# Turning expert 2's rows beside expert 1's first layer in an attention and mixture-of-experts kernel

## The chip, the cores and the metric

The kernel runs on one core of a Trainium2 chip. The metric is device time in microseconds (us), one launch. Engines in this text: TensorE (PE) multiplies, VectorE (DVE) and ScalarE (ACT) work on tiles, GpSimd (POOL) issues the indirect transfers, SyncE (SP) issues the others.

## The reference

A decayed linear attention over 4 x 8 heads and 768 positions gives `x` with 3072 tokens of 512. A noisy gate picks two of eight experts for each token, and each expert is a two-layer network:

```python
for e in range(E):
    for k in range(2):
        mask = top2[:, k] == e
        h = np.maximum(x[mask] @ w1[e], 0.0)
        out[mask] += top2_w[mask, k, None] * (h @ w2[e])
```

`w1[e]` is 512 x 1024, `w2[e]` 1024 x 512. Everything is fp32.

## The kernel before, in words

Attention, gate and routing come first; expert 0 is begun beside them. Then experts 1 to 7 run one after the other. An fp32 product is made of three products of split operands (high x high, high x low, low x high), so weights and activations are split into two parts: the high one by ScalarE, the low one by VectorE.

An expert has up to seven tiles of rows: six of 128, and a tail of 64 or 32 rows. Tiles 0 to 3 make the wide part, tiles 4 to 6 the narrow one. `parts` orders them: expert 1 does the wide part first, later experts the narrow one (`tile_order(2)` is 4, 5, 6, 0, 1, 2, 3). The loop at line 1133 runs the first layer: for each part eight blocks `f` of 128 hidden columns, each 12 matmuls into a bank `pS` (four of them) and an eviction with relu, ScalarE first (line 863), then VectorE (line 867). The loop at line 1161 runs the second layer, `gemm2`: for each tile 24 matmuls (16 for the tail) into `pO` or `pKV` by turns, an eviction by VectorE (line 907) into a buffer `ot`, and a scatter to `out` by POOL.

The rows of the next expert come on this way, with one tile `xg` per row tile:

- `gather_rows`: POOL gathers the tokens' rows of `x` into `xg` (line 810), by lists that `prepare` loads with `load_rec` (line 801).
- `turn_rows`: VectorE transposes 32 x 32 blocks into a buffer `ot` (line 829), and SyncE stores it to `turned` in DRAM (line 831). The pool `ot` has three buffers, shared with the evictions of the second layer.
- `fetch_rows`: four SyncE transfers bring the blocks back transposed into `xg` (line 836).
- `split_rows`: ScalarE writes the high part `xth` (line 843), VectorE the low part `xtl` (line 844).

Each engine and SyncE's queue works in the order in which the program issues. From expert 2 on, turning and fetching lie in the wide half of the first layer, and splitting in the second layer. Expert 1's successor is different: its rows are gathered in expert 1's narrow half (line 1155), and turned, fetched and split in its second layer (lines 1169 to 1174), a fetch one tile behind its turn. Weight loads share SyncE: in step `t` of the second layer, `split_w(1, e + 1, t)` splits a piece of the next expert's first weights and `load_w(2, e + 1, t)` loads a piece of its second ones into the buffer `wst` set free. The last row tile of expert 2 (`late`) is fetched after the second layer and split inside expert 2's own first layer (line 1143).

Beside all that VectorE computes a small table for overflowing rows (`ovj`), a step at a time, on lines 1081 to 1117.

Of the kernel before, what the change touches and what calls it, by code (L numbers as in the profile page):

```python
# [39 lines left out]
FB = F // 128  # L40
# [38 lines left out]
def tiles(e):  # L79

    return NT if TAILS[e] else NT - 1


def size(e, t):
    return TS if t < NT - 1 else TAILS[e]


def sub(ap, offset, dims):
    return bass.AP(tensor=ap.tensor, offset=ap.offset + offset, ap=dims)
# [27 lines left out]
def kernel(  # L117
# [557 lines left out]
    def xt(part, c):  # L675

        i = c.start >= TX * TS
        return XT[part][i][:, :, c.start - i * TX * TS:c.stop - i * TX * TS]
# [95 lines left out]
    def parts(e):  # L774
        if not e:
            return [(sum(PARTS0[:i]), n) for i, n in enumerate(PARTS0)]
        n = PARTS1 if TAILS[e] else PARTS2
        return [(0, n[0]), (n[0], n[1])] if e == 1 else [(n[0], n[1]), (0, n[0])]

    def tile_order(e):  # L780

        return [t0 + t for t0, n in parts(e) for t in range(n)]
# [11 lines left out]
    def load_rec(e, i, queue=nc.sync):  # L794

        t0, n, size = list(lists(e))[i]
        nm = f"{i}{size}" if e else f"z{i}"
        r = rp.tile([size, n, RW], I32, name="rec" + nm, bufs=3 if e else 1)
        if e:
            rows = lst[bass.ds(ROW[e] + t0 * TS, n * size), :]  # L800
            queue.dma_start(r.rearrange("p n w -> p (n w)"), rows.rearrange("(p n) w -> p (n w)", p=size))
        else:
            ld = queue.dma_start(r, sub(lst, t0 * TS * RW, [[n * RW, size], [1, n * RW]]))
            if i < NG - 1:
                lst_ld.append((i, ld))
        for j in range(n):
            REC[e, t0 + j] = r[:, j, :]
    def gather_rows(e, t, rows=NTOK):
        at = REC[e, t][:, 0:1] if e else IDX[t // 2][:, t % 2:t % 2 + 1]
        nc.gpsimd.indirect_dma_start(  # L810
            out=XG[t][:size(e, t)], out_offset=None, in_=x_tok[:rows, :],
            in_offset=bass.IndirectOffsetOnAxis(ap=at, axis=0),
            bounds_check=rows - 1, oob_is_err=False)
# [12 lines left out]
    def turn_rows(t, n):  # L826

        tr = hp.tile([TS, DM], FT, name="ot", bufs=3)[:n, :]
        nc.vector.transpose(tr.rearrange("p (i d c) -> p i d c", d=DB, c=32),
                            XG[t][:n, :].rearrange("p (d i c) -> p i d c", d=DB, c=32))  # L830
        nc.sync.dma_start(turned[t][:n, :], tr)

    def fetch_rows(t, n):

        for i in range(4):
            nc.sync.dma_start(XG[t][i * 32:(i + 1) * 32, :4 * n].rearrange("r (b x) -> r b x", x=128),  # L836
                              sub(turned[t], i * 128, [[DM, 32], [32 * DM, n // 32], [1, 128]]))

    def split_rows(t, n):

        p = XG[t][:, :4 * n].rearrange("p (b d c) -> p d b c", d=DB, c=32)
        hi, lo = [xt(i, slice(t * TS, t * TS + n)).rearrange("p d (b c) -> p d b c", c=32) for i in range(2)]
        nc.scalar.activation(hi, p, AF.Copy)  # L843
        nc.vector.tensor_tensor(lo, p, hi.bitcast(FT), op=SUB)  # L844

    def gemm1(e, t0, n, f):
        evac1(e, t0, n, f, mm1(e, t0, n, f))

    def columns(e, t0, n):
        return slice(t0 * TS, min((t0 + n) * TS, FULL + TAILS[e]))  # L850
# [19 lines left out]
    def ht(e, part, f, c):  # L870

        at = c.start + (0 if not part else TAILS[e] if c.start >= FULL else CAP + TAIL)
        return HT[0][:, f, at:at + c.stop - c.start]
# [10 lines left out]
    def gemm2(e, t, between=None):  # L884
        n = size(e, t)
        cs = slice(t * TS, t * TS + n)
        p = psum.tile([128, DM], FT, name=("pO", "pKV")[next(turn) % 2])
        terms = [(f, a, b) for f in range(FB) for a, b in ((0, 0), (0, 1), (1, 0))]
        o = hp.tile([TS, DM], FT, name="ot", bufs=3) if e else PV[t]
        w, pv = REC[e, t][:, 1:2].bitcast(FT), PV[t][:n, :]  # L890
        if n == TS:
            for i, (f, a, b) in enumerate(terms):
                if between and i == MID:
                    between()
                nc.tensor.matmul(p, ht(e, a, f, cs), W2[b][f // 2][:, f % 2, :], start=(i == 0),  # L895
                                 stop=(i == len(terms) - 1))
        else:
            for i in range(2 * FB):
                f, b = i // 2, i % 2
                nc.tensor.matmul(p[:2 * n, :], HT[0][:, f, FULL:FULL + 2 * n], W2[b][f // 2][:, f % 2, :],  # L900
                                 start=(i == 0), stop=(i == 2 * FB - 1))
            o = o[:n, :]
            nc.scalar.activation(o, p[n:2 * n, :], AF.Copy)
            nc.vector.tensor_add(o, o, p[:n, :])
            p = o
        if e:
            nc.vector.scalar_tensor_tensor(o, p, w, pv, op0=MULT, op1=ADD)  # L907
            scatter_out(e, t, o)
        else:
            nc.vector.tensor_scalar(o, p, w, None, op0=MULT)  # L910

    def scatter_out(e, t, o):
        nc.gpsimd.memset(spacer, 0.0)
        st = nc.gpsimd.indirect_dma_start(  # L914
            out=out, out_offset=bass.IndirectOffsetOnAxis(ap=REC[e, t][:, 0:1], axis=0), in_=o, in_offset=None,
            bounds_check=NTOK - 1, oob_is_err=False)
        if t == 0:
            out_st.clear()
        for s in out_st:
            tc.declare_no_dep(st.ins, s.ins, reason="an expert has a token once")  # L920
        out_st.append(st)
# [199 lines left out]
    def prepare(e):  # L1121

        which_expert(e, nc.sync)
        which_list(e, nc.sync)
        for i, _ in enumerate(lists(e)):
            load_rec(e, i)

    for e in range(1, E):
        if e == E - 1:
            n_over = nc.values_load(ntot[0:1, 0:1], min_val=0, max_val=MAXOV)  # L1130
        if e == 1:
            prepare(2)
        for i, (t0, n) in enumerate(parts(e)):
            for f in range(FB):
                gemm1(e, t0, n, f)
                if e == 1 and f >= 4:
                    next(ovj, None)
                if e > 1 and i and e + 1 < E:
                    if 1 <= f <= tiles(e + 1):
                        fetch_rows(f - 1, size(e + 1, f - 1))  # L1140
                    if f < tiles(e + 1):
                        turn_rows(f, size(e + 1, f))
                if e == 2 and not i and f == 1:
                    split_rows(late, size(2, late))
                    gather_rows(3, late)
                if i == 0 and f % 2 == 0:
                    split_w(2, e, f // 2)
                if i == 0 and f % 2 and e + 1 < E:
                    load_w(1, e + 1, f // 2)
                if (t0 == 0 or e == 1) and f < tiles(e):  # L1150
                    nc.gpsimd.tensor_copy(spacer, ht(e, 0, f, columns(e, t0, n))[0:1, 0:1].bitcast(FT))  # L1151
                    if t0 == 0:
                        gather_prev(e, f)
                    else:
                        gather_rows(2, tile_order(2)[f])
        if e == E - 1:
            nc.gpsimd.drain()
        if e + 2 < E:
            prepare(e + 2)
        nxt = tile_order(e + 1) if e + 1 < E else []  # L1160
        for t in range(tiles(e)):
            gemm2(e, t)
            if e == 1:
                next(ovj, None)
            if e + 1 < E:
                if t < 4:
                    split_w(1, e + 1, t)
                    load_w(2, e + 1, t)
                for j in nxt[t - 1:t] if e == 1 and t else ():
                    fetch_rows(j, size(2, j))  # L1170
                for j in nxt[t:t + 1] if e == 1 else ():
                    turn_rows(j, size(2, j))
                for j in (nxt[t - 1:t] if t else ()) if e == 1 else nxt[t:t + 1]:
                    split_rows(j, size(e + 1, j))
                    if e + 2 < E and j < tiles(e + 2):
                        gather_rows(e + 2, j)
        if e == 1:
            late = nxt[-1]
            fetch_rows(late, size(2, late))
    with tc.For_i(0, n_over) as it:  # L1180
        e_r = nc.sync.value_load(tab[0:1, 0, bass.ds(it, 1)], min_val=0, max_val=E - 1)
        row = nc.sync.value_load(tab[0:1, 1, bass.ds(it, 1)], min_val=0, max_val=E * STRIDE - OV)
# [59 lines left out]
```

## Time and profile before

| | before |
|---|---|
| median of 3 runs | 738.89 us (736.31 to 739.82) |
| profiled execution, own time | 741.05 us |
| its span, first to last instruction | 739.3 us |
| TensorE busy | 706.7 us, 96% |
| VectorE busy | 357.6 us, 48% |
| ScalarE busy | 237.0 us, 32% |
| POOL busy | 274.9 us, 37% |
| mean granted TensorE clock | 0.989 of full speed |

The span starts at 0 in every view. A wait is the idle time of an engine just before an instruction, with the instruction that ended it. TensorE is busy nearly everywhere, so the places where it is not are to be found in its waits and its timeline; the other engines matter where TensorE waits for them. For a transfer the row shows its issue; the time to landing comes apart.

### The profile page before, as it was taken

What the parts mean: (1) busy time and instruction counts of PE and PEld (TensorE: products, weight loads), DVE (VectorE), ACT (ScalarE), POOL (GpSimd) and SP (SyncE); (2) the same over time, 40 slices, a digit from 0 to 9 for tenths busy, and PEclk for the clock granted to TensorE, in tenths of its full rate; (3) what the DMA queues carried; (4) which work ended last, traced back from release to release, by engine and by line L of the source; (5) the groups of instructions that cost most, each with busy time, mean ns of one, the idle gap of its engine ahead of it and who ended that gap; (6) DMA issues with size and microseconds to landing.
All of it is one profiled execution on the core that took longest, in us unless ns stands there. A gap on an engine that the chain in (4) does not pass through costs nothing.

```text
span 739.3 us, 13508 instructions
## 1 busy us (share of the span) xinstructions
PE 706.7 (96%) x4917; PEld 601.7 (81%) x4917; DVE 357.6 (48%) x815; ACT 237.0 (32%) x451; POOL 274.9 (37%) x439
## 2 busy tenths in 40 slices
PE   8899998899999999769999999999999999999996
PEld 6788886699888887658888887988798898889885
DVE  6335869777235543455436433644353544335211
ACT  1567685331133320142214221423042322224200
POOL 3200336677756442323252415242512433221311
PEclk9999999999999999989999999999999999999999
DMA  7999997981527636457464636564655556550211
GB/s 162 204 230 232 245 255 210 272 243 39 114 62 264 185 87 195 141 156 217 147 222 138 178 129 228 158 187 145 208 150 178 193 173 180 161 166 14 79 43 38
DMA packets 139594, 122.50 MB, mean 166 GB/s; under 512 B 88554, under 2 KB 107370, under 8 KB 139524
## 3 DMA queue, kind: packets, MB, share of 16 engines
q1 hardware_dynamic: 124996, 85.22, 43.7%
q0 software_dynamic: 13104, 36.34, 15.6%
q8 instruction: 40, 0.66, 0.4%
q14 instruction: 30, 0.25, 0.1%
q10 hardware_dynamic: 1424, 0.04, 0.1%
HBM read 87.15 MB, written 35.55 MB: 166 GB/s over the span
## 4 chain that ended last, share of the span: by engine, by line
PE 75%; DMA 9%; issue 6%; DVE 4%; ACT 2%; SPq 2%; POOL 1%; POOLq 0%; ACTq 0%; DVEq 0%
PE pS L857 34%; PE pKV L895 14%; PE pO L895 12%; DMA wst<-in_moe_w_dram 3%; DMA xg<-turned 2%; PE pS L356 2%; PE pKV L369 2%; PE pO L369 2%; PE pO L900 1%; PE pS L326 1%; PE pS L429 1%; SPq L836 1%; PE pS L401 1%; POOL out_dram L914 1%; DMA qt<-in_q_dram 1%
## 5 line engine op out<-in xcount | busy, mean ns | idle before, releaser
L857 PE MATMUL pS<-xth,w1h 128*128 128x512 f32 (+3 forms) x544 | 182.0, 335 | 7.7 <-DVE ht L867 5.8
L857 PE MATMUL pS<-xtl,w1h 128*128 128x512 f32 (+3 forms) x544 | 181.3, 333 | 0.4 <-DVE xtl L822 0.4
L857 PE MATMUL pS<-xth,w1l 128*128 128x512 f32 (+3 forms) x544 | 181.1, 333 | 0.0
L863 ACT ACTIVATE ht<-pS 128x512 fp32r<-128x512 f32 (+3 forms) x136 | 65.6, 483 | 218.7 <-PE pS L857 213.0
L867 DVE SCALAR_TENSOR_TENSOR ht<-pS,ht 128x256 fp32r<-128x256 f32 (+3 forms) x176 | 76.5, 455 | 112.1 <-ACT ht L863 110.1
L895 PE MATMUL pO<-w2h,ht 128*128 128x512 f32 x384 | 124.1, 394 | 3.9 <-DVE ot L907 3.9
L895 PE MATMUL pKV<-w2h,ht 128*128 128x512 f32 x384 | 123.0, 391 | 0.0
L857 PEld LDWEIGHTS pS<-xth,w1h 128*128 128x128 f32 x544 | 103.5, 190 | 17.6 <-ACT ht L863 6.0
L857 PEld LDWEIGHTS pS<-xtl,w1h 128*128 128x128 f32 x544 | 103.5, 190 | 9.4 <-DVE xtl L822 0.7
L857 PEld LDWEIGHTS pS<-xth,w1l 128*128 128x128 f32 x544 | 103.5, 190 | 8.9
L914 POOL DMA_INDIRECT out_dram<-ot,rec x46 | 59.2, 1286 | 118.3 <-DVE ot L907 110.3
L895 PEld LDWEIGHTS pO<-w2h,ht 128*128 128x128 f32 x384 | 72.8, 190 | 20.7 <-DVE ot L907 4.3
L895 PEld LDWEIGHTS pKV<-w2h,ht 128*128 128x128 f32 x384 | 72.1, 188 | 16.2
L810 POOL DMA_INDIRECT xg<-x_tok,rec x46 | 49.4, 1074 | 91.3 <-DVE xtl L844 45.5
L895 PE MATMUL pO<-w2l,ht 128*128 128x512 f32 x192 | 76.0, 396 | 0.0
L895 PE MATMUL pKV<-w2l,ht 128*128 128x512 f32 x192 | 75.4, 393 | 0.0
L879 POOL DMA_INDIRECT pv<-out_dram,rec x46 | 47.1, 1023 | 31.7 <-issue 25.2
L843 ACT ACTIVATE xth<-xg 128x512 fp32r<-128x512 f32 (+1 forms) x39 | 22.4, 598 | 105.5 <-DMA xg<-turned 105.5
L622 POOL DMA_INDIRECT lst<-recs,dest x48 | 47.7, 993 | 13.6 <-issue 9.0
L844 DVE TENSOR_TENSOR xtl<-xg,xth 128x512 fp32r<-128x512 f32 (+1 forms) x39 | 25.6, 656 | 46.7 <-ACT xth L843 46.7
L1151 POOL COPY spacer<-ht 1x1 f32<-1x1 f32 x53 | 9.4, 177 | 99.6 <-ACT ht L863 99.5
L907 DVE SCALAR_TENSOR_TENSOR ot<-pKV,rec,pv 128x512 f32<-128x512 f32 x21 | 15.8, 750 | 59.8 <-PE pKV L895 57.1
(228 smaller groups left out, 932.3 us busy)
## 6 DMA issues: line engine op xcount, KB each, us to landing
wst<-in_moe_w_dram SPq DMA_DIRECT2D x48, 512.0 KB, 4.6
turned<-ot SPq DMA_DIRECT2D x36, 256.0 KB, 3.1
xg<-turned SPq DMA_DIRECT2D x144, 64.0 KB, 2.1
wst<-in_moe_w_dram SPq DMA_DIRECT2D x32, 256.0 KB, 4.0
kt<-in_k_dram SPq DMA_DIRECT2D x24, 256.0 KB, 5.2
qt<-in_q_dram SPq DMA_DIRECT2D x24, 256.0 KB, 5.5
vt<-in_v_dram SPq DMA_DIRECT2D x24, 256.0 KB, 5.3
x_tok<-xc SPq DMA_DIRECT2D x12, 512.0 KB, 5.4
```

What stands on the lines that cost most here:

```text
L369: nc.tensor.matmul(PO[u][a][half(g), hp, :], lhs, rhs, start=n == 1, stop=n == (8 if u % NW or a else 4))
L622: st = nc.gpsimd.indirect_dma_start(out=lst, out_offset=bass.IndirectOffsetOnAxis(ap=r["dest"][:, i, c:c + 1], axis=0), in_=r["rec"][:, c, ...
L810: nc.gpsimd.indirect_dma_start(out=XG[t][:size(e, t)], out_offset=None, in_=x_tok[:rows, :], in_offset=bass.IndirectOffsetOnAxis(ap=at, ax ...
L843: nc.scalar.activation(hi, p, AF.Copy)
L844: nc.vector.tensor_tensor(lo, p, hi.bitcast(FT), op=SUB)
L857: nc.tensor.matmul(p, W1[a][d][:, fs], xt(b, cs)[:, d], start=(d == 0 and i == 0), stop=(d == DB - 1 and i == 2))
L863: nc.scalar.activation(ht(e, 0, f, cs), p, AF.Relu)
L867: nc.vector.scalar_tensor_tensor(ht(e, 1, f, c), p[:, r], 0.0, ht(e, 0, f, c).bitcast(FT), op0=OP.max, op1=SUB)
L879: nc.gpsimd.indirect_dma_start(out=PV[t][:size(e, t), :], out_offset=None, in_=out, in_offset=bass.IndirectOffsetOnAxis(ap=REC[e, t][:, 0: ...
L895: nc.tensor.matmul(p, ht(e, a, f, cs), W2[b][f // 2][:, f % 2, :], start=(i == 0), stop=(i == len(terms) - 1))
L907: nc.vector.scalar_tensor_tensor(o, p, w, pv, op0=MULT, op1=ADD)
L914: st = nc.gpsimd.indirect_dma_start(out=out, out_offset=bass.IndirectOffsetOnAxis(ap=REC[e, t][:, 0:1], axis=0), in_=o, in_offset=None, bo ...
```

## The change

Expert 2's rows are turned from block 3 (`LAG`) of expert 1's narrow half on. `turn_next(k)` fetches the row tile at place `k - 2` of `tile_order(2)` and turns the one at place `k`. It is called after blocks 3 to 7 (k = 0 to 4) and ahead of each tile of expert 1's second layer (k = 5 and on). Each row tile is now split one step earlier in the second layer, as for later experts, the last one in its last step; the steps for `late` are gone.

```diff
--- before.py
+++ after.py
@@ -1125,6 +1125,16 @@
         for i, _ in enumerate(lists(e)):
             load_rec(e, i)
 
+    LAG = 3
+
+    def turn_next(k):
+
+        js = tile_order(2)
+        for j in js[k - 2:k - 1] if k >= 2 else ():
+            fetch_rows(j, size(2, j))
+        for j in js[k:k + 1]:
+            turn_rows(j, size(2, j))
+
     for e in range(1, E):
         if e == E - 1:
             n_over = nc.values_load(ntot[0:1, 0:1], min_val=0, max_val=MAXOV)
@@ -1140,9 +1150,8 @@
                         fetch_rows(f - 1, size(e + 1, f - 1))
                     if f < tiles(e + 1):
                         turn_rows(f, size(e + 1, f))
-                if e == 2 and not i and f == 1:
-                    split_rows(late, size(2, late))
-                    gather_rows(3, late)
+                if e == 1 and i and f >= LAG:
+                    turn_next(f - LAG)
                 if i == 0 and f % 2 == 0:
                     split_w(2, e, f // 2)
                 if i == 0 and f % 2 and e + 1 < E:
@@ -1159,6 +1168,8 @@
             prepare(e + 2)
         nxt = tile_order(e + 1) if e + 1 < E else []
         for t in range(tiles(e)):
+            if e == 1:
+                turn_next(t + FB - LAG)
             gemm2(e, t)
             if e == 1:
                 next(ovj, None)
@@ -1166,17 +1177,10 @@
                 if t < 4:
                     split_w(1, e + 1, t)
                     load_w(2, e + 1, t)
-                for j in nxt[t - 1:t] if e == 1 and t else ():
-                    fetch_rows(j, size(2, j))
-                for j in nxt[t:t + 1] if e == 1 else ():
-                    turn_rows(j, size(2, j))
-                for j in (nxt[t - 1:t] if t else ()) if e == 1 else nxt[t:t + 1]:
+                for j in nxt[t:t + 1]:
                     split_rows(j, size(e + 1, j))
                     if e + 2 < E and j < tiles(e + 2):
                         gather_rows(e + 2, j)
-        if e == 1:
-            late = nxt[-1]
-            fetch_rows(late, size(2, late))
     with tc.For_i(0, n_over) as it:
         e_r = nc.sync.value_load(tab[0:1, 0, bass.ds(it, 1)], min_val=0, max_val=E - 1)
         row = nc.sync.value_load(tab[0:1, 1, bass.ds(it, 1)], min_val=0, max_val=E * STRIDE - OV)
```

SyncE's queue in expert 1's second layer before, from the first store on (`wst` is a weight piece, `turned_364` the stored tile 4, `xg_2430` its place in SBUF, 365 and 2432 tile 5):

```order
L831 DMA turned_364<-ot 128x512
L748 ISA
L748 DMA wst<-in_moe_w_dram 128x2x512
L836 DMA xg_2430<-turned_364 32x4x128 x4
L831 DMA turned_365<-ot 128x512
L748 ISA
L748 DMA wst<-in_moe_w_dram 128x2x512
L836 DMA xg_2432<-turned_365 32x4x128 x4
```

and the changed kernel's, from the same store, which now lies in the first layer's narrow half:

```order
L831 DMA turned_364<-ot 128x512
L831 DMA turned_365<-ot 128x512
L836 DMA xg_2430<-turned_364 32x4x128 x4
L831 DMA turned_366<-ot 32x512
L836 DMA xg_2432<-turned_365 32x4x128 x4
L831 DMA turned_360<-ot 128x512
L836 DMA xg_2434<-turned_366 32x128 x4
L831 DMA turned_361<-ot 128x512
```

The stores and the first three fetches now come in a row, ahead of the lists of expert 3 and of the four weight loads that stood between them. After the lists follow fetch and store alternately with the weight loads: fetches four and five of `xg` stand ahead of the first and second weight load.

VectorE in expert 1's narrow half, blocks 3 and 4 (line 867 evicts, 1091 and 1093 are the table):

```order
 L867 SCALAR_TENSOR_TENSOR ht<-pS,ht 128x256
 L867 SCALAR_TENSOR_TENSOR ht<-pS,ht 128x64
+L829 STREAM_TRANSPOSE ot<-xg_2430 128x512
 L867 SCALAR_TENSOR_TENSOR ht<-pS,ht 128x256
 L867 SCALAR_TENSOR_TENSOR ht<-pS,ht 128x64
 L1091 COPY ov_3463<-ov_3462 1x8
 L1093 TENSOR_TENSOR ov_3463<-ov_3463,ov_3462 1x1 x4
+L829 STREAM_TRANSPOSE ot<-xg_2432 128x512
```

A turn stands behind the eviction and the table step of its block, and ahead of the next block's eviction.

VectorE in the second step of expert 1's second layer (line 907 is the tile's eviction, 772 the weight split, 844 a row split):

```order
 L907 SCALAR_TENSOR_TENSOR ot<-pO,rec_3186,pv_2425 128x512
 L1104 TENSOR_REDUCE ovt<-ovg 1x40
 L772 TENSOR_TENSOR w1l_334<-wst,w1h_330 128x1024
-L829 STREAM_TRANSPOSE ot<-xg_2432 128x512
-L844 TENSOR_TENSOR xtl_348<-xg_2430,xth_346 128x4x128
+L844 TENSOR_TENSOR xtl_348<-xg_2432,xth_346 128x4x128
 L907 SCALAR_TENSOR_TENSOR ot<-pKV,rec_3186,pv_2427 128x512
```

The turn is gone from here, and the row split is that of the next row tile, a step earlier than before.

## Rows read from the trace of the kernel before

**Rows 1.** The waits of TensorE, whole run: engine, line, releaser: total us, times, longest.

```profile
PE pS L857 <- DVE ht L867: 5.8, 1, 5.8
...
PE pO L895 <- DVE ot L907: 3.9, 1, 3.9
...
PE pKV L900 <- DVE ot L907: 1.6, 1, 1.6
PE pS L857 <- ACT w2h L768: 1.5, 1, 1.5
```

**Rows 2.** Timeline of TensorE, 252.7 to 404.8: start, us, line, operation.

```profile
252.79 0.30 PE L857 MATMUL pS<-xth,w1h 128*128 128x320 f32 x1
...
266.87 0.40 PE L895 MATMUL pKV<-w2h,ht 128*128 128x512 f32 x1
...
311.21 0.29 PE L857 MATMUL pS<-xth,w1h 128*128 128x288 f32 x1
...
333.43 0.39 PE L857 MATMUL pS<-xth,w1h 128*128 128x512 f32 x1
...
355.20 0.39 PE L895 MATMUL pO<-w2h,ht 128*128 128x512 f32 x1
...
391.82 0.29 PE L857 MATMUL pS<-xth,w1h 128*128 128x288 f32 x1
...
404.46 0.39 PE L857 MATMUL pS<-xth,w1h 128*128 128x512 f32 x1
```

**Rows 3.** Windows: us, busy PE, PEld, DVE, ACT, POOL, PEclk, DMA share, GB/s.

```profile
303.50:333.40 29.90, 20.96 (x122) 18.95 (x122) 14.57 (x32) 9.53 (x17) 8.25 (x11) 0.89 0.53 162
355.20:391.80 36.60, 36.60 (x161) 29.19 (x160) 13.70 (x18) 7.54 (x11) 14.37 (x18) 1.00 0.53 177
```

**Rows 4.** Timeline of VectorE, expert 1's second layer.

```profile
287.11 0.69 DVE L844 TENSOR_TENSOR xtl<-xg,xth 128x512 fp32r<-128x512 f32 x1 [6.16 <-ACT xth L843]
...
297.02 0.69 DVE L844 TENSOR_TENSOR xtl<-xg,xth 128x512 fp32r<-128x512 f32 x1 [6.42 <-ACT xth L843]
```

**Rows 5.** Timeline of SyncE, expert 1's second layer.

```profile
290.01 0.41 SPq L748 DMA_DIRECT2D wst<-in_moe_w_dram  x1
290.53 1.92 SPq L836 DMA_DIRECT2D xg<-turned  x4
292.56 0.42 SPq L831 DMA_DIRECT2D turned<-ot  x1
```

**Rows 6.** Timeline of ScalarE, the last row tiles.

```profile
321.56 0.63 ACT L843 ACTIVATE xth<-xg 128x512 fp32r<-128x512 f32 x1 [4.64 <-DMA xg<-turned]
```

**Rows 7.** Timeline of VectorE, a turn in expert 2's wide half.

```profile
337.60 0.70 DVE L829 STREAM_TRANSPOSE ot<-xg 128x512 f32<-128x512 f32 x1
```

**Rows 8.** Timeline of VectorE, expert 1's narrow half.

```profile
262.31 0.56 DVE L867 SCALAR_TENSOR_TENSOR ht<-pS,ht 128x256 fp32r<-128x256 f32 x2 [1.21 <-ACT ht L863]
...
262.96 0.71 DVE L1093 TENSOR_TENSOR ov<-ov,ov 1x1 f32<-1x1 f32 x4
```

**Rows 9.** Timeline of POOL, expert 1's narrow half.

```profile
256.16 1.05 POOL L810 DMA_INDIRECT xg<-x_tok,rec  x1 [0.61 <-issue]
```

**Rows 10.** Transfers into `xg`, 255 to 270.

```profile
DMA to landing us min/median/max: 3.4/3.5/3.5
```

**Rows 11.** Transfers into `pv`, 333 to 356, expert 2's wide half.

```profile
DMA to landing us min/median/max: 2.9/3.9/4.4
```

**Rows 12.** Timeline of SyncE, expert 2's second layer.

```profile
368.05 1.71 SPq L836 DMA_DIRECT2D xg<-turned  x4
371.18 1.53 SPq L801 DMA_DIRECT2D rec<-lst  x3
372.91 6.76 SPq L748 DMA_DIRECT2D wst<-in_moe_w_dram  x4
```

**Rows 13.** Transfers to and from `turned`, 262 to 325.

```profile
DMA to landing us min/median/max: 1.8/3.7/5.0
```

**Rows 14.** Transfers into `wst`, 266 to 300.

```profile
DMA to landing us min/median/max: 4.3/4.3/4.3
```

## The prediction

> **What bounds the kernel now.** I read the waits of TensorE first. It is busy for almost the whole span, so only what stops it can be won. Its longest waits are few, and four of them are neighbours: 5.8, 3.9, 1.6 and 1.5 us [rows 1]. The timeline of TensorE puts all four between expert 1's second layer and the end of expert 2's first pass: the second layer starts at 266.87, expert 2's narrow half at 311.21, its wide half at 333.43 [rows 2]. The same work one expert later is the yardstick, because nothing stops TensorE there: it starts at 355.20, 391.82 and 404.46 [rows 2]. The matmuls are as many: six tiles of 24 and a tail of 16, then 8 blocks of 12 with 288 columns.
>
> - Second layer: 44.34 us for expert 1, 36.62 for expert 2, so 7.72 lost.
> - Narrow half: 22.22 us for expert 2, 12.64 for expert 3, so 9.58 lost.
>
> Together 17.30 us are lost, 2.3% of the run, of which 12.8 are the four waits. The rest is the clock: its mean is 0.89 of full speed from 303.5 to 333.4 and 1.00 in the yardstick [rows 3]. Full speed is 2.4 GHz; the mean falls because part of that stretch, after the stops, ran at 1.2.
>
> The reader should next see why it stops. On VectorE the split of fetched rows (line 844) at 297.02 comes after an idle 6.42 us [rows 4]. Behind it in VectorE's order stands the eviction of a second-layer bank (line 907), which TensorE needs. The split waits for ScalarE's half (line 843), which waits for the fetch. On SyncE the fetch stands behind a weight load: the load goes out at 290.01, the fetch at 290.53 [rows 5]. The weight load had waited for VectorE's weight split, itself behind an eviction. So eviction, weight split, weight load, fetch, row split and the next eviction form a ring. Row splits at 287.11 and 297.02 are 9.91 us apart [rows 4]; a tile of TensorE needs 36.62 x 24/160 = 5.49. The late row tile is worse: ScalarE waits 4.64 us for a fetch at 321.56 [rows 6], with expert 2's first eviction behind it. The 5.8 us wait comes from there.
>
> **The change, part by part.** No work is added or removed: seven turns, seven stores, 28 fetches, seven row splits, all moved.
>
> *Five turns go into expert 1's narrow half, after its blocks 3 to 7 (counted from 0), two to the first tiles of its second layer.* A turn costs 0.70 us [rows 7]. A narrow block takes TensorE (266.87 - 252.79)/8 = 1.76 us [rows 2]. In it VectorE evicts for 0.56 us and then does table work, 0.8 at the most (262.87 to 263.67) [rows 8]. With a turn that worst block comes to 2.06, so VectorE falls some half a microsecond behind by block 7. Four PSUM banks let TensorE run ahead of it, and the second layer uses other banks. I cost this at nothing. Without that cover all five turns exposed would cost 3.5 us, the upper end; there is no gain below nothing, since TensorE does not wait in this half today.
>
> *Do the gathered rows arrive in time?* POOL issues the first gather at 256.16, for 1.05 us [rows 9], and one more with each block; they land within 3.5 us [rows 10]. Counted from the end of the issue, the first lands by 260.7; the first turn can start near 261.1, behind block 3's eviction, and each later pair keeps that distance. Beside stores, fetches and weight loads in expert 2's wide half, POOL's gathers took up to 4.4 us [rows 11]; then every turn is some half a microsecond late, once and not five times, and the banks hide that too. I take nothing, with the difference of 0.9 as the upper end.
>
> *Stores and fetches on SyncE.* A store takes 0.4 us to issue [rows 5], a fetch's four transfers 1.7 [rows 12], together 2.1 against the block's 1.76; and each fetch waits for its store to land, 3.7 us in the middle and 5.0 at the worst now [rows 13]. The first three fetches come ahead of expert 3's list loads and of every weight load. With the first store at 261.8 the first fetch goes out near 265.5. Three rounds of 2.1 bring SyncE to 272. The list loads with their register loads take 3.2 us more (369.76 to 372.91 in the yardstick [rows 12]), so the fourth fetch goes out at 275, the fifth behind the first weight load at 278. The sixth and seventh stand behind the second and third weight loads, hence behind weight splits at 281 and 286, my estimate from evictions at 278.1 and 283.6. With 5.0 us to land the last is there by 293. Its split is due after the tail, at 266.87 + 36.62 = 303.5, that of the sixth after six tiles, at 299.8. At least 10 us spare.
>
> *Weight loads of expert 2's second layer* go out behind fetches, the first near 278, the last near 292. In the yardstick they start only at 372.91 [rows 12], 18.9 us before the pass that splits them, without a TensorE wait. Here the last has 11 us before 303.5. No cost; if that cover went, a wait like the present 1.5 us one [rows 1].
>
> *The ring of three buffers* is shared by turns and evictions. The first eviction (272.6) takes the buffer of the fourth turn, whose store lands by my estimate near 273.5; the second (278.1) that of the sixth turn, near 281. The second may wait 3 us, while its PSUM bank is wanted only when the fourth tile starts, at 283.3. Behind it wait a weight split and the next row split, both with slack. No cost, 1.5 us as the upper end.
>
> *The late row tile* is split in the second layer's last step, no longer between expert 2's evictions. That removes the 5.8 us wait, provided its fetch is early, as above.
>
> *The Trainium skill's view.* Its page "DMA: Bandwidth & Descriptors", section "Issuing engines are not separate DMA queues", says that transfers from SP, ACT and POOL run on the same 16 engines and interleave, which speaks against putting five stores among the gathers. The trace agrees: 4.4 against 3.5 us [rows 10, 11]. By the uncrowded row the sum is 17.30; by the rule each turn starts late, the banks hide it, and the sum stays while rival B becomes likelier.
>
> **Sum.** 7.72 + 9.58 = 17.30 us gained, nothing paid. The profiled execution took 741.05 us (span 739.3), so it would take 723.75. It lies 2.16 above the median of 738.89; for the median I get 721.6, and say **722**, with half a microsecond for small waits.
>
> **Rivals.**
> - **B, half of it.** If evictions still wait behind row splits, 7.72 stays lost: 738.89 - 9.58 = 729.3. If only the late tile is still late, 9.58 stays lost: 731.2. For it: SyncE becomes the tightest queue, and the transfers share engines. Against: 10 us spare.
> - **C, the wait is passed on.** Expert 2's narrow half waits for all four weight loads, 4.3 us to land each [rows 14]: 17.2 back, 738.8. For it: the weight loads move behind fetches, and a wait on a weight split exists. Against: the later loads of the yardstick.
> - **D, slower.** The ring closes on every tile. Place: SyncE's order in the second layer, where a fetch stands behind a weight load that waits for VectorE. It decides if a fetch goes out less than a tile ahead of its split. Then seven steps run at 9.91 us: 69.4 against 44.34 now, 25.0 worse, less the 9.58 of the narrow half: 754. Against: the first four fetches stand ahead of every weight load, and each later one behind a load of four tiles earlier.
>
> That the change doesn't do what it says is no case: each engine's order shows the moves.
>
> **How the numbers follow.** Forecast 0.89, B 0.06, C 0.02, D 0.03. Only differences over 0.5%, 3.7 us, can be told from none. Forecast and B are faster, 0.95; C is the same, 0.02; D slower, 0.03. The range begins at 718.5: 721.6 less the 2.6 us by which the lowest run lies under the median, and half a microsecond. It ends at 727: the forecast with 3.5 us for exposed turns and 1.5 for the buffers. B, C and D lie beyond, 0.11 left out; the ends' own uncertainty is the rest.
>
> **What would show it.** Right: TensorE's waits on the evictions of lines 907 and 867 are gone from the list; second layer near 36.6 us, narrow half near 12.6, both at clock 1.00; turns in expert 1's narrow half at 0.70 us; row splits one per tile. Wrong: a narrow half of expert 1 longer than 14.1 us; row splits still some 9.9 us apart; TensorE waiting for a weight split.

## The result and the profile after

The changed kernel takes 721.25 us (719.55 to 722.43, 4 runs) against 739.34 for the kernel before: ratio 0.9769, 95% interval 0.9747 to 0.9791, that is 15.5 to 18.7 us less. The forecast was 722.

The waits of TensorE over the whole run of the changed kernel, the longest and that of the second layer, answer to [rows 1]:

```profile
PE pS L356 <- DVE qTs L333: 1.9, 1, 1.9
...
PE pKV L895 <- DVE ot L907: 0.7, 1, 0.7
```

None of the four waits of before is there; a new one of 0.7 us is. The timeline of TensorE, at the starts that [rows 2] shows for the kernel before:

```profile
249.21 0.30 PE L857 MATMUL pS<-xth,w1h 128*128 128x320 f32 x1
...
263.29 0.40 PE L895 MATMUL pKV<-w2h,ht 128*128 128x512 f32 x1
...
286.11 0.50 PE L895 MATMUL pKV<-w2h,ht 128*128 128x512 f32 x1 [0.67 <-DVE ot L907]
...
300.87 0.29 PE L857 MATMUL pS<-xth,w1h 128*128 128x288 f32 x1
...
313.51 0.39 PE L857 MATMUL pS<-xth,w1h 128*128 128x512 f32 x1
```

Expert 1's narrow half takes 263.29 - 249.21 = 14.08 us, as before. Its second layer takes 37.58 instead of 44.34, expert 2's narrow half 12.64 instead of 22.22, which is the yardstick's. From the start of the narrow half to that of expert 2's wide half it is 64.30 us instead of 80.64: 16.34 gained. The windows answer to [rows 3] (us, busy PE, PEld, DVE, ACT, POOL, PEclk, DMA share, GB/s):

```profile
249.20:263.30 14.10, 14.10 (x98) 14.08 (x97) 8.97 (x33) 3.68 (x8) 7.61 (x15) 1.00 0.57 161
263.30:300.90 37.60, 36.94 (x163) 29.99 (x162) 17.70 (x30) 7.71 (x11) 20.33 (x19) 1.00 0.70 213
300.90:313.50 12.60, 12.60 (x97) 12.60 (x96) 9.37 (x23) 7.74 (x13) 2.33 (x4) 1.00 0.54 157
```

The clock is full in all three windows. In the two profiled executions the span fell by more, from 739.3 to 719.5 us: 3.58 us of that lie ahead of expert 1's narrow half (252.79 to 249.21), in code that the change does not touch. In the later runs the same code reached that place anywhere from 249.1 to 262.8 us. So what follows compares this stretch, not spans, and times only as ratios within a comparison.

VectorE in expert 1's narrow half:

```profile
256.97 0.56 DVE L867 SCALAR_TENSOR_TENSOR ht<-pS,ht 128x256 fp32r<-128x256 f32 x2 [1.20 <-ACT ht L863]
257.44 0.70 DVE L829 STREAM_TRANSPOSE ot<-xg 128x512 f32<-128x512 f32 x1
...
260.03 0.69 DVE L829 STREAM_TRANSPOSE ot<-xg 128x512 f32<-128x512 f32 x1
260.66 0.50 DVE L867 SCALAR_TENSOR_TENSOR ht<-pS,ht 128x256 fp32r<-128x256 f32 x2
...
264.01 0.56 DVE L867 SCALAR_TENSOR_TENSOR ht<-pS,ht 128x256 fp32r<-128x256 f32 x2 [0.17 <-ACT ht L863]
264.48 0.46 DVE L1100 TENSOR_REDUCE ovt<-ovg 1x40 f32<-1x320 f32 x1
264.87 0.69 DVE L829 STREAM_TRANSPOSE ot<-xg 128x512 f32<-128x512 f32 x1
```

The first turn stands at 257.44, right behind block 3's eviction, and waits for no gather. Turns take 0.69 to 0.70 us, as [rows 7] had it, and block 7's eviction is at 264.01 after 0.17 us idle: VectorE has caught up.

### The profile page after: what moved, and what is told of

Its sections match the earlier page's. It is cut to its first block, busy times and chain, and to the rows that moved or that the text cites. A ratio compares the mean times of both kernels' runs of the same rounds, so it can differ in the third digit from the quotient of the medians.

```text
span 719.5 us, 13510 instructions
## 1 busy us (share of the span) xinstructions
PE 701.0 (97%) x4917; PEld 598.4 (83%) x4917; DVE 357.3 (50%) x815; ACT 238.2 (33%) x451; POOL 279.8 (39%) x439
## 4 chain that ended last, share of the span: by engine, by line
PE 80%; issue 5%; DMA 5%; DVE 5%; SPq 2%; POOL 1%; ACT 1%; POOLq 0%; DVEq 0%; ACTq 0%
PE pS L857 36%; PE pKV L895 15%; PE pO L895 14%; PE pS L356 3%; DMA vt<-in_v_dram 2%; PE pKV L369 2%; PE pO L369 2%; PE pO L900 2%; PE pS L429 1%; DMA out_dram<-ot,rec 1%; PE pKV L900 1%; PE pS L326 1%; PE pS L313 1%; POOL out_dram L914 1%; PE pS L819 1%
## 5 line engine op out<-in xcount | busy, mean ns | idle before, releaser
L914 POOL DMA_INDIRECT out_dram<-ot,rec x46 | 61.4, 1335 | 124.7 <-DVE ot L907 107.4
L810 POOL DMA_INDIRECT xg<-x_tok,rec x46 | 50.9, 1106 | 58.3 <-DMA rec<-lst 14.2
L907 DVE SCALAR_TENSOR_TENSOR ot<-pO,rec,pv 128x512 f32<-128x512 f32 x21 | 15.8, 750 | 59.6 <-PE pO L895 57.2
```

The lines of the kernel that those rows point to most:

```text
L810: nc.gpsimd.indirect_dma_start(out=XG[t][:size(e, t)], out_offset=None, in_=x_tok[:rows, :], in_offset=bass.IndirectOffsetOnAxis(ap=at, ax ...
L914: st = nc.gpsimd.indirect_dma_start(out=out, out_offset=bass.IndirectOffsetOnAxis(ap=REC[e, t][:, 0:1], axis=0), in_=o, in_offset=None, bo ...
```

## The experiments

The table gives each run's two times that matter, from TensorE's timeline as above, in us. "Order" is whether the fetches of the second layer stand ahead of the weight load of their step or behind it, "lead" how many steps of the second layer lie between a row tile's turn and its split. With a lead of 1 or 2 the fetch stands in the step of the split, with 5 three steps ahead of it. In late_split the lead of 5 holds for all row tiles but the last, which is split later still.

| run | order | lead | second layer, expert 1 | narrow half, expert 2 | ratio to before |
|---|---|---|---|---|---|
| before | behind | 1 | 44.34 | 22.22 | 1 |
| order_only | ahead | 1 | 37.00 | 24.52 | 0.9948 (0.9915 to 0.9982) |
| lag6_behind | behind | 2 | 53.48 | 12.65 | 0.9971 (0.9955 to 0.9988) |
| lag6 | ahead | 2 | 36.64 | 12.64 | 0.9738 (0.9693 to 0.9783) |
| lag6_again | ahead | 2 | 36.64 | 12.64 | 0.9776 (0.9750 to 0.9802) |
| loads_behind | behind | 5 | 36.63 | 12.64 | 0.9754 (0.9702 to 0.9806) |
| changed kernel | ahead | 5 | 37.58 | 12.64 | 0.9769 (0.9747 to 0.9791) |
| after_again | ahead | 5 | 38.11 | 12.64 | 0.9779 (0.9755 to 0.9803) |
| late_split | ahead | 5 | 38.75 | 12.64 | 0.9767 (0.9713 to 0.9821) |
| in_place | ahead | 5 | 36.64 | 12.64 | 0.9778 (0.9737 to 0.9819) |

Expert 1's narrow half took 14.07 or 14.08 us in every run.

**order_only**, the kernel before with one move:

```diff
+                for j in nxt[t - 1:t] if e == 1 and t else ():
+                    fetch_rows(j, size(2, j))
                 if t < 4:
                     split_w(1, e + 1, t)
                     load_w(2, e + 1, t)
-                for j in nxt[t - 1:t] if e == 1 and t else ():
-                    fetch_rows(j, size(2, j))
```

> The kernel before, with only the fetch of a row tile issued ahead of the weight load of its step; turns stay in the second layer. My theory (turn, store, fetch and row split of one tile are too long for a step, so the turns must come early): taking the weight load out of the ring helps the second layer by some 4 to 7 us of its 7.7, and the late tile still costs expert 2's narrow half most of its 9.6, so 732 to 736 us. Rival, the order on SyncE is all that mattered: 722. Rival, only the early turns matter: 739.

The order alone takes 7.34 of the 7.72 us off the second layer, a little more than I expected. But 2.30 of them come back in expert 2's narrow half, which takes 24.52 instead of 22.22; over both 5.04 us are gained. TensorE, then ScalarE, then VectorE of this run:

```profile
273.43 0.40 PE L895 MATMUL pKV<-w2h,ht 128*128 128x512 f32 x1
...
310.43 0.29 PE L857 MATMUL pS<-xth,w1h 128*128 128x288 f32 x1
...
326.94 0.58 PE L857 MATMUL pS<-xth,w1h 128*128 128x288 f32 x1 [10.03 <-DVE ht L867]
...
334.95 0.39 PE L857 MATMUL pS<-xth,w1h 128*128 128x512 f32 x1
```

```profile
290.74 0.63 ACT L843 ACTIVATE xth<-xg 128x512 fp32r<-128x512 f32 x1 [14.74 <-DMA xg<-turned]
...
325.01 0.63 ACT L843 ACTIVATE xth<-xg 128x512 fp32r<-128x512 f32 x1 [6.14 <-DMA xg<-turned]
325.66 0.41 ACT L863 ACTIVATE ht<-pS 128x288 fp32r<-128x288 f32 x1
...
329.50 0.63 ACT L843 ACTIVATE xth<-xg 128x512 fp32r<-128x512 f32 x1 [2.19 <-DMA xg<-turned]
```

```profile
314.85 0.74 DVE L907 SCALAR_TENSOR_TENSOR ot<-pO,rec,pv 128x512 f32<-128x512 f32 x1
```

Without the weight load the ring is shorter, but not gone. The first of the seven row splits is at 290.74 and the last at 329.50, 6.46 us apart in the mean, and TensorE needs 5.49 for a tile. So VectorE falls behind: it evicts the sixth tile at 314.85, when TensorE has been in expert 2's narrow half since 310.43. TensorE does not wait in the second layer, and meets the delay behind it. ScalarE still waits 6.14 us for a fetch at 325.01 with expert 2's evictions behind it, and 2.19 for the last one at 329.50; TensorE waits 10.03. The last two row tiles are turned only in the second layer's last steps (at 315.71 and 320.82). The ratio shows a small gain.

**loads_behind**, the changed kernel with the fetches of the second layer behind the weight load:

```diff
             if e == 1:
-                turn_next(t + FB - LAG)
+                turn_next(t + FB - LAG, False)
...
                     load_w(2, e + 1, t)
+                if e == 1:
+                    fetch_next(t + FB - LAG)
```

> The changed kernel, with the fetches of the second layer (the fourth to seventh) issued behind the weight load of their step instead of ahead of it. My theory (a lead of three to four tiles makes the order unimportant): 721 to 722.5 us, second layer within 1 us of the changed kernel's 37.6, no new wait of TensorE over 1 us. Rival, the order on SyncE is what gained: at least 5 us slower than the changed kernel, 726 or more.

As expected: with a lead of 5 the order changes nothing for the worse. The second layer is 0.95 us shorter than the changed kernel's, because its third eviction waits for no scatter; in_place below takes that up. Of the two parts of the change, the early turns and the fetches ahead of the weight loads, the second earns nothing at this lead. With a lead of 2 it does (lag6_behind).

**late_split** puts the last tile's split back to its old place:

```diff
-                for j in nxt[t:t + 1]:
+                for j in nxt[t:t + 1] if e > 1 or t < NT - 1 else ():
...
+                if e == 2 and not i and f == 1:
+                    split_rows(tile_order(2)[-1], TS)
+                    gather_rows(3, tile_order(2)[-1])
```

> The changed kernel, with the last row tile split again between expert 2's evictions (after its block 1), as before. My theory (the rows came late, the place of the split did no harm): 721 to 722 us, expert 2's narrow half within 0.5 us of 12.64. Rival, the place of the split made the 9.6 us: 728 to 731, the narrow half 20 us or more.

The narrow half stays at 12.64: for the last row tile it was the late rows, not the place of their split. The second layer is 1.2 us longer than the changed kernel's, by a wait that the next run explains, on VectorE's timeline:

```profile
296.48 0.75 DVE L907 SCALAR_TENSOR_TENSOR ot<-pKV,rec,pv 128x512 f32<-128x512 f32 x1 [7.12 <-DMA out_dram<-ot,rec]
```

**in_place** lets a full tile's eviction overwrite its own gathered partial sum, so that it needs no shared buffer:

```diff
-        o = hp.tile([TS, DM], FT, name="ot", bufs=3) if e else PV[t]
+        o = hp.tile([TS, DM], FT, name="ot", bufs=3) if e and n < TS else PV[t]
```

> The changed kernel, with the evictions of the second layer written over the gathered partial sums, so that only turns and tails use the three shared buffers. My theory (VectorE's waits for scatters in the second layer are waits for a shared buffer, and one of them made TensorE's 0.67 us wait): no wait of line 907 on a scatter, second layer 36.6 us instead of 37.6, 720.3 us. Rival, the buffers are not it, POOL and the transfers are simply late: second layer still 37 us or more, 721.3.

First the evictions of the changed kernel on VectorE, then those of this one:

```profile
269.83 0.75 DVE L907 SCALAR_TENSOR_TENSOR ot<-pKV,rec,pv 128x512 f32<-128x512 f32 x1 [1.13 <-DMA turned<-ot]
...
275.79 0.75 DVE L907 SCALAR_TENSOR_TENSOR ot<-pO,rec,pv 128x512 f32<-128x512 f32 x1 [2.47 <-DMA out_dram<-ot,rec]
...
285.30 0.75 DVE L907 SCALAR_TENSOR_TENSOR ot<-pKV,rec,pv 128x512 f32<-128x512 f32 x1 [6.65 <-DMA out_dram<-ot,rec]
```

```profile
276.93 0.75 DVE L907 SCALAR_TENSOR_TENSOR pv<-pKV,rec,pv 128x512 f32<-128x512 f32 x1 [0.32 <-PE pKV L895]
...
282.42 0.75 DVE L907 SCALAR_TENSOR_TENSOR pv<-pO,rec,pv 128x512 f32<-128x512 f32 x1 [1.99 <-PE pO L895]
...
287.92 0.75 DVE L907 SCALAR_TENSOR_TENSOR pv<-pKV,rec,pv 128x512 f32<-128x512 f32 x1 [2.63 <-PE pKV L895]
```

In the changed kernel the first eviction waits 1.13 us for a store, the second 2.47 and the third 6.65 us for the scatter of an earlier eviction; the third ends at 286.05, and TensorE starts its fifth tile at 286.11 instead of some 285.3 (263.29 and four tiles of 5.49). Without the shared buffer each eviction waits for TensorE alone, and the second layer is at the yardstick's 36.6. loads_behind and lag1 reach the same 36.6 with the shared buffers: there the third eviction waits for TensorE only. The 0.94 us are 0.13% of the run, which the times cannot show.

**lag6** changes one number, so that only two turns lie in the narrow half and a fetch goes out in the step of its split:

```diff
-    LAG = 3
+    LAG = 6
```

> The changed kernel with LAG = 6: only two turns lie in expert 1's narrow half, and each fetch goes out in the very step in which its rows are split, behind the weight load of the step before. This is the point from which rival D was to decide. By my later reading of the rows the ring then spans two tiles: eviction 0.75, table 0.5, weight split 1.2, fetch 1.9, landing 4, row split 1.3 make about 9.7 us against 2 x 5.49, so TensorE still hardly waits: second layer 36.6 to 39 us, ratio to before within 0.005 of the changed kernel's 0.977. Rival D: the ring closes at 9.9 us a step, second layer 60 us or more, ratio over 1.

> LAG = 6 once more. Second layer 36.6 us, 1 us less than the changed kernel, which is 0.13% and not to be told from it in the times: ratio within 0.003 of the changed kernel's. Rival, the earlier LAG = 6 time shows a real gain of 0.3%: ratio 0.974 or less, below the changed kernel's interval.

The ring does not close at the point that rival D named: the first fetch of the second layer goes out at 279.49 and its split starts at 284.27, less than a tile later. Two turns in the narrow half are as good as five. The first ratio, 0.9738, did not repeat: beside the changed kernel on one chip it is 0.9776 against 0.9779.

**lag6_behind** is LAG = 6 with the edit of loads_behind.

> The changed kernel with LAG = 6 and the fetches of the second layer behind the weight load of their step: rows are fetched in the step in which they are split, behind a weight load that waits for VectorE, as in the kernel before; the last row tile is turned two steps earlier than there. My theory (order and lead replace each other in the second layer, only the lead helps the last tile): second layer 43 to 48 us as before, narrow half of expert 2 below 14, ratio to before about 0.987. Rival, with early turns the order never matters: second layer 36.6, ratio 0.975. Rival, ring D: every step 9.9 us, second layer 60 us or more.

Here the ring does close. ScalarE's row splits:

```profile
281.34 0.63 ACT L843 ACTIVATE xth<-xg 128x512 fp32r<-128x512 f32 x1 [12.60 <-DMA xg<-turned]
...
291.49 0.63 ACT L843 ACTIVATE xth<-xg 128x512 fp32r<-128x512 f32 x1 [8.56 <-DMA xg<-turned]
...
301.83 0.31 ACT L843 ACTIVATE xth<-xg 128x128 fp32r<-128x128 f32 x1 [8.77 <-DMA xg<-turned]
...
311.47 0.63 ACT L843 ACTIVATE xth<-xg 128x512 fp32r<-128x512 f32 x1 [8.39 <-DMA xg<-turned]
```

They are 10.15, 10.34 and 9.64 us apart, like the 9.91 of the kernel before. On SyncE each weight load, which waits for VectorE's weight split, stands right ahead of the fetch of the same step:

```profile
285.49 0.41 SPq L748 DMA_DIRECT2D wst<-in_moe_w_dram  x1
286.01 2.03 SPq L836 DMA_DIRECT2D xg<-turned  x4
...
295.64 0.41 SPq L748 DMA_DIRECT2D wst<-in_moe_w_dram  x1
296.15 1.95 SPq L836 DMA_DIRECT2D xg<-turned  x4
```

The second layer takes 53.48 us, 9 more than the kernel before, where the ring ran for three steps and not for all four that have a weight load. I had expected 43 to 48, and a ratio of 0.987 instead of 0.9971. Yet the narrow half is at 12.65. Here TensorE itself is late, which gives the last rows time; but lag6, where it is not, has the same 12.64, so two steps of lead are enough for them. Each half of the loss can thus stand without the other.

**double_turn** and **quad_turn** repeat each of the five turns in the narrow half, into the same buffer:

```diff
-            turn_rows(j, size(2, j))
+            turn_rows(j, size(2, j), 4 if k < 5 else 1)
```

> The changed kernel with each of the five turns in expert 1's narrow half done twice into the same buffer, 3.5 us more on VectorE. The last four blocks use the banks that blocks 0 to 3 left, all evicted ahead of the first turn, so no turn can stop TensorE in this half; the next eviction that it needs has to be done by about 11 us after the half. My theory: narrow half 14.1 us, second layer below 39. Rival, the turns are exposed one for one: 3.5 us more.

> The same with each of the five turns done four times, 10.5 us more on VectorE. My theory: the narrow half stays at 14.1 us, and as VectorE's slack of some 8 us before the second layer's third tile is used up, the second layer grows to 40 to 46 us. Rival, VectorE has room for that too: below 38.5. Rival, the turns stop the narrow half: over 16 us there.

Doubled turns leave the second layer at 36.98 us, quadrupled ones take it to 43.84; the narrow half stays at 14.08 and 14.07, expert 2's at 12.63 and 12.64. VectorE with quadrupled turns (the line numbers are one higher):

```profile
265.05 0.56 DVE L868 SCALAR_TENSOR_TENSOR ht<-pS,ht 128x256 fp32r<-128x256 f32 x2 [1.20 <-ACT ht L864]
265.52 2.94 DVE L830 STREAM_TRANSPOSE ot<-xg 128x512 f32<-128x512 f32 x4
268.39 0.52 DVE L868 SCALAR_TENSOR_TENSOR ht<-pS,ht 128x256 fp32r<-128x256 f32 x2
...
280.09 0.52 DVE L868 SCALAR_TENSOR_TENSOR ht<-pS,ht 128x256 fp32r<-128x256 f32 x2
```

Block 7's eviction comes at 280.09, 8.7 us after TensorE left the half at 271.37, and TensorE has not waited there. The price appears in the second layer, as two waits of 2.58 and 2.48 us on evictions (the first ahead of the third tile, which starts at 285.12) and a clock of 0.83 in the stretch of the first (282.4 to 292.3).

**lag1** and **lag0** move the turns forward.

> The changed kernel with LAG = 1: the first turn stands behind block 1 and waits some 3 us for its gather, with the evictions of later blocks behind it. My theory: the banks hide that, narrow half of expert 1 14.1 to 14.5 us, second layer 36.6 to 38.5. Rival, the wait for the gathers is exposed: narrow half 16 us or more.

> The changed kernel with LAG = 0: the first turn stands right behind block 0 and waits for its gather, about 4.9 us, with the evictions of the next blocks behind it. Four banks cover three blocks, 5.3 us. My theory: the narrow half of expert 1 grows from 14.1 to 14.5 to 16.5 us and the second layer stays below 38. Rival, a wait for the gather costs its full length in every turn: 20 us or more. Rival, early turns are free wherever they stand: 14.1.

With LAG = 1 the first turn waits for its gather and the evictions queue behind it, hidden as expected (VectorE):

```profile
258.49 0.71 DVE L829 STREAM_TRANSPOSE ot<-xg 128x512 f32<-128x512 f32 x1 [2.06 <-DMA xg<-x_tok,rec]
259.12 0.52 DVE L867 SCALAR_TENSOR_TENSOR ht<-pS,ht 128x256 fp32r<-128x256 f32 x2
260.28 0.71 DVE L829 STREAM_TRANSPOSE ot<-xg 128x512 f32<-128x512 f32 x1 [0.64 <-DMA xg<-x_tok,rec]
```

Second layer 36.64 us. LAG = 0 tells nothing on gathers: its turns stand ahead of the gathers in the program, so it turns the rows that lay in `xg` before and waits for none. Its times, 14.08 and 36.64, show only that turns at this place cost nothing.

**after_again** is the changed kernel, beside lag6_again.

> The changed kernel once more, beside LAG = 6 on the same chip. Second layer 36.6 to 39 us, by how long the eviction waits for a scatter in its shared buffer; ratio to before 0.975 to 0.979.

Its third eviction waited 6.54 us for a scatter and stopped TensorE for 1.20; the ratio is that of the first time, 0.9779 against 0.9769.

## Why the prediction was right, point by point

- **What bounds it.** Right but for one reading. The forecast of 17.30 us came to 16.34 in the stretch: 9.58 of 9.58 in the narrow half, 6.76 of 7.72 in the second layer. The clock came back with the waits.
- **The number.** That 721.25 lies within 1 us of the 722 is in part luck. The stretch gave 16.34, the medians differ by 18.09. The other 1.75 lie outside it: in the profiled pair 3.58 us lay ahead of the stretch, in code that the change does not touch.
- **The ring.** Right in its parts, and settled by lag6_behind, where it closes at 10 us a step. order_only shows that the weight load is one member of it: without it a row split comes every 6.46 us, still more than TensorE's 5.49. I had not seen that this alone would nearly free the second layer, nor that its delay would be handed on to the narrow half. Only the early turns do for both.
- **The late row tile.** Here the prediction read a row wrongly. It took ScalarE's split at 321.56 [rows 6] for that of the late row tile. It is the sixth of the seven, which the kernel before splits in the second layer's last step; the late tile's is the seventh, at 328.07. VectorE, then ScalarE, kernel before:

```profile
322.22 0.69 DVE L844 TENSOR_TENSOR xtl<-xg,xth 128x512 fp32r<-128x512 f32 x1 [2.65 <-ACT xth L843]
322.82 0.52 DVE L867 SCALAR_TENSOR_TENSOR ht<-pS,ht 128x256 fp32r<-128x256 f32 x2
```

```profile
328.07 0.63 ACT L843 ACTIVATE xth<-xg 128x512 fp32r<-128x512 f32 x1 [4.20 <-DMA xg<-turned]
```

TensorE's 5.8 us wait ended at 323.49, with the eviction at 322.82 behind the sixth tile's split. So moving the late tile's split could not have removed it, as the prediction says it would; that split stands ahead of the 1.5 us wait, which ended at 330.00. What removed both is that both tiles are turned early, so the forecast of 9.58 us held. The place of the sixth tile's split is no rival: in the changed kernel the seventh tile's split stands there and waits for nothing (ScalarE):

```profile
301.57 0.62 ACT L843 ACTIVATE xth<-xg 128x512 fp32r<-128x512 f32 x1
```

- **Turns beside the narrow half.** Nothing paid, right, and for a simpler reason than the one I gave. With LAG = 3 the first turn stands behind block 3's eviction, so all four banks that blocks 4 to 7 need are free before any turn: even quadrupled turns did not stop this half. The cover is the time up to the second layer's third tile, where quad_turn shows the first wait. "Half a microsecond behind by block 7" was too much: that eviction had to wait 0.17 us for ScalarE.
- **Gathers in time.** Right. None was waited for.
- **SyncE.** The last fetch went out at 288.12, behind the third weight load at 287.60, which is 24.3 us after the second layer's start; I had put the weight split ahead of it at 19.1, and it stood behind the eviction that waited 6.65 us. The spare time covered that: the row split behind it, at 301.57, waited for nothing. From the timeline of SyncE, changed kernel:

```profile
287.60 0.41 SPq L748 DMA_DIRECT2D wst<-in_moe_w_dram  x1
288.12 1.93 SPq L836 DMA_DIRECT2D xg<-turned  x4
```

- **The ring of three buffers.** This step failed, without harm to the forecast. I took the buffers to go round in the order of the program, so that the second eviction would follow the sixth turn. The trace shows the second, third and fifth eviction waiting for the scatters of evictions before them (2.47, 6.65 and 2.65 us), where I had put 3 on the second and nothing on the others. in_place shows the cost, 0.94 us, inside the 1.5 that I had allowed.
- **The signs named.** One eviction of line 907 is still in the list of waits, with 0.67 us. Two row splits on VectorE are 9.51 us apart, at 277.99 and 287.50, but not by the ring: the eviction that waited 6.65 us for a scatter stands between them.
- **The rule of the Trainium skill** on shared engines (page "DMA: Bandwidth & Descriptors", section "Issuing engines are not separate DMA queues"). The trace is in line with it, and no run isolates it: with a DMA share of 0.70 in the second layer, against 0.46 before, transfers from or to `turned` landed within 7.1 us at the most, against 5.0 [rows 13]. The gathers beside the stores took 3.8 in the middle, against 3.5 [rows 10]. No row came late for it, because of the lead.
- **Rivals.** B, in its second form, is what order_only shows: the second layer without the narrow half. C did not come: the last weight load went out at 290.64, 10.2 us ahead of expert 2's first layer, and TensorE waited for no weight split. D named the right place and step time, but a wrong point: what closes the ring is a fetch behind the weight load of its own step, not a fetch less than a tile ahead of its split, for lag6 has that and runs free.

## What to carry to other kernels

When engines work in program order, write down who waits for whom around one step, and compare that ring with the step of the bounding engine: taking one slow member out shortens it, and a lead of some steps opens it. Look behind the phase too: a phase that no longer waits may have handed its delay on to the next. A delay at the end of a phase needs the lead; here no order of the queue repaired rows that were turned too late. Before putting work between evictions, count which of them the next blocks still need: behind the last needed one it cannot stop these blocks, and costs only what it delays later (here nothing for five turns, 7 us in the second layer when each was done four times).

## What was not expected of the hardware

Scatters to `out` landed in 4.2, 5.5 and 6.8 us (least, middle, most) in the changed kernel's second layer, and in 3.1, 5.8 and 6.3 before; so they are not much slower, but evictions now wait for them. POOL took 2.74 us to issue the first of them and 1.01 for a later one; in the kernel before the first took 2.13. The changed kernel's two, then that of the kernel before:

```profile
270.86 2.74 POOL L914 DMA_INDIRECT out_dram<-ot,rec  x1 [6.65 <-DVE ot L907]
...
291.68 1.01 POOL L914 DMA_INDIRECT out_dram<-ot,rec  x1 [0.21 <-issue]
```

```profile
273.61 2.13 POOL L914 DMA_INDIRECT out_dram<-ot,rec  x1 [5.84 <-DVE ot L907]
```

Beside the issue at 270.86 VectorE ran a weight split of 1.20 us and a row split of 0.67, beside that at 273.61 a weight split of 1.20 and no row split, and beside that at 291.68 no split. The issue is 1.73 and 1.12 us longer than the quiet one, nearly the time of the splits. A split that begins well into an issue does not lengthen it: at 303.44 in the changed kernel, with a row split from 303.71, the issue took 0.94. So the rows speak for the overlap, rather than for crowded DMA engines, as what lengthens the issue; no run tried it.
